# Routed experts after a Fourier filter: weight splits queued one by one, and a penalty added by ScalarE instead of GpSimd

## The chip, the cores and the metric

The kernel runs on one core of a Trainium2 chip. The metric is the device time of one execution in microseconds (us). Engine names are those of the profile: PE (TensorE matmuls), PEld (its weight loads), DVE (VectorE), ACT (ScalarE), POOL (GpSimd), SP (SyncE).

## What is computed

The input `x` (8 x 2496 x 256, float32) is filtered along its sequence in the frequency domain, and the 19968 resulting tokens go through eight experts. Each (token, expert) pair has a logit. Pairs are taken in falling order of their logits, over all tokens and experts at once; a token is given to the expert of the pair if it has none yet and the expert has fewer than 2496 tokens. Then each expert runs two matrix products with a relu between them on its own tokens.

```
y = irfft(rfft(x, axis=1) * (filt_r + 1j*filt_i))       # 8 x 2496 x 256
logits = y @ w_gate                                     # 19968 x 8
for idx in argsort(-logits.flatten()):                  # greedy, capacity 2496 per expert
    tok, e = idx // 8, idx % 8
    if assigned[tok] < 0 and counts[e] < 2496: assigned[tok] = e; counts[e] += 1
out[assigned == e] = relu(y[assigned == e] @ w1[e]) @ w2[e]   # w1: 256x1024, w2: 1024x256
```

## The kernel before

**Stages.** Up to about 530 us the kernel computes the Fourier filter as matrix products (class `Fft`) and the logits `lg`, a tile of 117 x 176 x 8 in SBUF whose last index is the expert. From there on the eight experts run one after another (class `Ffn`, `run`). While expert number e computes, the routing of the next one (class `Route`) is woven into the same instruction streams.

**The experts.** An expert's 2496 tokens come in five groups `g` of 512 (the last of 448). For each group, eight first products (`first`, line 850) write `pz`, a PSUM tile of 128 x 512. Four such buffers exist, and the transposes of gathered tokens (`turn`, `ptr`, line 828) share them. ACT makes the high part of the relu from `pz` (line 856, the relu copy), and DVE the low part (`hl`, lines 864 and 867), which frees the buffer. Each matrix operand is split into a high and a low part in this way, so that three matmuls give the precision of one in full float32. The second products (line 897) sum 24 matmuls into `py` for each 128 tokens; ACT copies `py` to `y` (line 907), and POOL scatters `y` to the output rows (line 908).

**The next expert's weights.** `Ffn.weights` loads both raw matrices by indirect DMAs from POOL (line 793). `split` turns them into high and low parts in eight pieces of 128 x 512 (parts 0 to 3 are of the first matrix, 4 to 7 of the second): ACT casts the high part (line 807; parts 0 to 3 read with a step of 8 elements), then POOL subtracts it from the raw piece (line 808). In `emit` a piece is taken from the list `split` after every fourth step of the expert's program; a step is one `yield` of `run`, and a second product of 128 tokens has four. The list is emptied at the hook `last`, in the last group. A piece's place in the program is not its place in the engine's queue: a scheduler orders the instructions of all engines but PE, and it moves them to where it expects them to be ready.

**The routing of the next expert.** `Route.phase` finds, in eleven rounds of counting, which expert closes next and its threshold. Then DVE computes the penalty `pen` for the closed expert (line 687), and POOL adds it to all logits in one instruction (line 718; 1408 elements per partition); the first reader afterwards is the maximum at line 635. The line is queued after the weight loads (`issue_after(s.wdma)`). The list of tokens is made by `places` in five chunks: DVE prepares bounds (lines 699 to 712, 747) and for each chunk a 0/1 matrix `OH` (lines 748, 749), which PE multiplies with a table (`rt`, line 755). Those matmuls stand at fixed places between the expert's own: PE's order is written by hand (`manual_schedule`), and PE waits where an operand is late.

```python
nc.scalar.copy(hi, src)                                                      # 807
(nc.gpsimd if e or part >= 4 else nc.vector).tensor_tensor(lo, src, hi...)   # 808
if split and n % 4 == 0: W.split(*split.pop(0))                              # 1031
```

Of the kernel before, what the change touches and what calls it, by code (L numbers as in the profile page):

```python
# [16 lines left out]
S = B * G  # L17
# [3 lines left out]

LAGS = [(1.6, 1.2), (1.9, 1.2), (2.4, 1.4), (2.2, 1.3), (2.2, 1.2), (2.6, 1.2), (2.6, 1.2), (2.6, 1.2)]
LO, M0, M1, M7 = (4.2, 1.2, 1.4), 3.5, 4.9, 6.9
TU0, TU = 1.1, 1.15
ORD, TF = (1, 0, 0, 1), (3, 5)
I1, FS, C0 = 5, -1, -4.4
V1, V1D, V2, V3, VP, I2, AC = 8, 0.5, 3, 2, -1, 5, 6.5
# [433 lines left out]
class Route:  # L461
# [166 lines left out]
    def phase(s, ph):  # L628
# [85 lines left out]
        yield 'w', 1.5  # L714
        if ph == 7:
            return
        with s.tc.issue_after(s.wdma) if ph else nullcontext():
            nc.gpsimd.tensor_tensor(s.lg, s.lg, pen[:117].unsqueeze(1).to_broadcast([117, S, 8]), op=OP.add)
        with s.tc.issue_after(s.last):
            t, t3 = v("u", [117, S]), v("u2", [117, S])  # L720
            nc.vector.scalar_tensor_tensor(s.asg, mem, 50.0, s.asg, op0=OP.mult, op1=OP.add)
# [53 lines left out]
class Ffn:  # L775
# [58 lines left out]
    def run(s, e, pump, hook):  # L834
# [7 lines left out]
        def first(g, f):  # L842
            n = min(512, CAP - 512*g)
            xh, xl = s.xT[e, g]
            p = s.ps.tile([128, 512], F32, name="pz", tag="c", bufs=4)
            m = 0
            for k in range(2):
                sl = slice(1024*k+128*f, 1024*k+128*f+128)
                for w, x in ((w1h, xh), (w1h, xl), (w1l, xh)):
                    nc.tensor.matmul(p[:, :n], w[:, sl], x[:, k, :n], start=m == 0, stop=m == 5)  # L850
                    m += 1
                yield 0.65 * n / 512
            hl = s.wp.tile([128, 1024], F32R, name="hl", bufs=NH)
            hs.setdefault(g, []).append(hl)
            h, l = (hl[:, 512*k:512*k+512] for k in range(2))
            nc.scalar.activation(h[:, :n], p[:, :n], AF.Relu)  # L856
            if f % 2 == 1 and f < 7 and 0 < g < 4 and s.busy():
                r = s.wp.tile([128, 512], F32, name="hr", bufs=2)
                nc.scalar.activation(r[:, :n], p[:, :n], AF.Relu)
                nc.gpsimd.tensor_tensor(l[:, :n], r[:, :n], h[:, :n].bitcast(F32), op=OP.subtract)  # L860
            else:

                if g < 4:
                    nc.vector.scalar_tensor_tensor(l[:, :n], p[:, :n], 0.0, h[:, :n].bitcast(F32), op0=OP.max, op1=OP.subtract)  # L864
                else:
                    for a, b, c in ((384, n, n), (0, 384, 512)):
                        nc.vector.scalar_tensor_tensor(hl[:, c:c+b-a], p[:, a:b], 0.0, h[:, a:b].bitcast(F32), op0=OP.max, op1=OP.subtract)
# [13 lines left out]
        for g in range(5):  # L881
            n = min(512, CAP - 512*g)
            yield from firsts(g, 8)
            if g == 4:
                hook('last')
            for t in range(4):
                if g < 4:
                    yield from firsts(g + 1, ORD[t])
                w = min(128, n - 128*t)
                p = s.ps.tile([128, D], F32, name="py", tag="b", bufs=2)  # L890
                half = w == 64
                hi, lo, both = slice(128*t, 128*t+w), slice(512+128*t, 512+128*t+w), slice(384, 512)
                terms = ((both, w2h), (hi, w2l)) if half else ((hi, w2h), (hi, w2l), (lo, w2h))
                m = 0
                for f in range(8):
                    for a, b in terms:
                        nc.tensor.matmul(p[:a.stop-a.start], hs[g][f][:, a], b[:, 256*f:256*f+256],  # L897
                                         start=m == 0, stop=m == 8 * len(terms) - 1, skip_group_check=half)
                        m += 1
                    if f in ((3,) if half else (1, 3, 5)):  # L900
                        yield 0.65
                y = s.wp.tile([128, D], F32, name="y", bufs=4)
                if half:
                    nc.scalar.copy(y[:w], p[w:])
                    nc.vector.tensor_tensor(y[:w], p[:w], y[:w], op=OP.add)
                else:
                    nc.scalar.copy(y, p)  # L907
                st = nc.gpsimd.indirect_dma_start(  # L908
                    out=out_rows, out_offset=bass.IndirectOffsetOnAxis(ap=ids[1][:w, 4*g+t:4*g+t+1], axis=0),
                    in_=y[:w], in_offset=None)  # L910
                for o in s.scat:
                    s.tc.declare_no_dep(st.ins, o.ins, reason="each token has one place")
                s.scat.append(st)
                if t in (1, 2) and g == 4:
                    hook(t)
                yield 0.65


def emit(tc, i, out):
    nc = tc.nc  # L920
    with ExitStack() as st:
# [89 lines left out]
        with tc.issue_after(R.last):  # L1011
            while split:
                W.split(*split.pop(0))
        n = 0
        with tc.manual_schedule(engines={mybir.EngineType.PE}):
            for e in range(8):
                pump.limit = e + 1
                def hook(what):
                    if isinstance(what, tuple):
                        gather(e, what[1])  # L1020
                    elif e < 7:
                        if what == 'last':
                            gather(e + 1, 0)
                            while split:
                                W.split(*split.pop(0))
                        else:
                            W.turn(e + 1, 0, what - 1)
                for pe in W.run(e, pump, hook):
                    pump.feed(pe)
                    n += 1  # L1030
                    if split and n % 4 == 0:
                        W.split(*split.pop(0))


class Pump:
# [80 lines left out]
```

## Time and profile before

| what | value |
|---|---|
| median of 3 runs | 1607.03 us (1606.12 to 1614.62) |
| the profiled execution | 1623.63 us, span 1621.9 us |
| mean granted TensorE clock | 0.944 |
| busy share PE, DVE, ACT, POOL | 88%, 62%, 43%, 40% |

The profile is of one execution that took 1.0% longer than the median of the runs. Times in a timeline count from the first instruction; "idle before" names what ended an engine's idle time. [...]

### The profile page before, as it was taken

To read this page: it belongs to the slowest core of one execution; us is meant where nothing else is said; L and a number is where in the kernel's file an instruction comes from. 1 tells how busy PE (TensorE), PEld (TensorE's weight loads), DVE (VectorE), ACT (ScalarE), POOL (GpSimd) and SP (SyncE) were. 2 spreads that over 40 slices of the span, in tenths; PEclk is the share of its full clock that TensorE was granted. 3 is DMA by queue.
4 is the path that set the end of the run, shared out by engine and by line. 5 is a ranking of instruction groups with operands and counts; after the bars stand their busy time and mean duration, and the time that the engine had idled before them with its cause. 6 is when DMAs were issued, how large, how long until landed. Compare 5 with 4: busy or idle time off the path is not lost. (4 is left out here: it accounts for less than half of the span.)

```text
span 1621.9 us, 27429 instructions
## 1 busy us (share of the span) xinstructions
PE 1435.0 (88%) x10374; PEld 1254.6 (77%) x10374; DVE 1012.4 (62%) x2560; ACT 702.2 (43%) x1647; POOL 643.7 (40%) x624
## 2 busy tenths in 40 slices
PE   2888777899887799899899799799799799999998
PEld 2887667799554588789788688788688688899898
DVE  3667656687447667766966777876886862422322
ACT  4556445566445433442533343442453343533322
POOL 0233212345111643743744554634744633523311
PEclk9999888999889899899999899899899999999999
DMA  9978879736987211110210121111211221111100
GB/s 148 159 111 167 197 166 179 127 79 148 236 262 265 80 35 69 56 43 24 85 56 31 69 64 39 69 46 48 80 43 45 80 88 34 54 41 40 53 27 25
DMA packets 121096, 148.74 MB, mean 92 GB/s; under 512 B 70630, under 2 KB 93756, under 8 KB 118660
## 3 DMA queue, kind: packets, MB, share of 16 engines
q1 hardware_dynamic: 97994, 70.63, 22.0%
q0 software_dynamic: 17840, 60.34, 11.4%
q10 hardware_dynamic: 5129, 16.01, 2.8%
q8 instruction: 82, 1.34, 0.4%
q14 instruction: 51, 0.41, 0.1%
HBM read 84.47 MB, written 62.50 MB: 91 GB/s over the span
## 5 line engine op out<-in xcount | busy, mean ns | idle before, releaser
L897 PE MATMUL py<-w1h,hl 128*128 128x256 f32 x2496 | 491.8, 290 | 23.1 <-DVE hl L864 20.2
L897 PEld LDWEIGHTS py<-w1h,hl 128*128 128x128 f32 x2496 | 408.4, 194 | 27.0 <-DVE hl L864 20.8
L897 PE MATMUL py<-w1l,hl 128*128 128x256 f32 (+1 forms) x1280 | 362.7, 285 | 0.0
L908 POOL DMA_INDIRECT out<-y,oid x160 | 170.5, 1065 | 406.9 <-ACT y L907 358.3
L856 ACT ACTIVATE hl<-pz 128x512 fp32r<-128x512 f32 (+1 forms) x320 | 186.6, 587 | 231.5 <-PE pz L850 192.9
L850 PE MATMUL pz<-xo,w0h 128*128 128x512 f32 (+1 forms) x640 | 268.0, 419 | 10.4 <-DVE hl L864 3.6
L850 PE MATMUL pz<-z,w0h 128*128 128x512 f32 (+1 forms) x640 | 251.0, 392 | 1.2 <-issue 1.0
L850 PE MATMUL pz<-xo,w0l 128*128 128x512 f32 (+1 forms) x640 | 251.4, 393 | 0.0
L897 PEld LDWEIGHTS py<-w1l,hl 128*128 128x128 f32 (+1 forms) x1280 | 245.0, 191 | 1.9
L864 DVE SCALAR_TENSOR_TENSOR hl<-pz,hl 128x512 fp32r<-128x512 f32 x227 | 155.1, 686 | 120.6 <-ACT hl L856 118.0
L814 POOL DMA_INDIRECT xg<-xs,xid x160 | 169.0, 1056 | 123.0 <-PE ptr L828 43.3
L907 ACT COPY y<-py 128x256 f32<-128x256 f32 x152 | 56.6, 372 | 328.0 <-PE py L897 267.4
L850 PEld LDWEIGHTS pz<-xo,w0h 128*128 128x128 f32 x640 | 124.1, 194 | 32.3 <-issue 7.1
L230 POOL TENSOR_TENSOR P<-P 128x256 f32<-128x256 f32 x80 | 59.7, 747 | 205.8 <-DVE P L228 204.8
L850 PEld LDWEIGHTS pz<-xo,w0l 128*128 128x128 f32 x640 | 122.4, 191 | 24.4
L207 PE MATMUL p<-cS,xr 117*128 117x120 f32 x688 | 107.2, 304 | 36.1 <-ACT xr L195 30.7
L850 PEld LDWEIGHTS pz<-z,w0h 128*128 128x128 f32 x640 | 123.6, 193 | 17.5 <-issue 1.5
L215 ACT COPY Y<-p 64x240 f32<-64x240 f32 (+1 forms) x304 | 116.0, 382 | 43.5 <-PE p L207 37.8
L207 PEld LDWEIGHTS p<-cS,xr 117*128 117x128 f32 x688 | 99.2, 219 | 43.2 <-ACT xr L195 30.7
L550 DVE TENSOR_TENSOR Gm<-M,thr 117x1232 bf16<-117x1232 f32 (+2 forms) x80 | 104.4, 1315 | 0.2
L759 ACT ACTIVATE junka<-rt,loc 128x176 bf16<-128x176 f32 x160 | 65.1, 407 | 70.0 <-DVE loc L756 55.4
L222 PE MATMUL p<-cW,Y 128*128 128x128 f32 x640 | 92.6, 280 | 1.9 <-DVE Q L229 1.9
(235 smaller groups left out, 2374.7 us busy)
## 6 DMA issues: line engine op xcount, KB each, us to landing
xt<-x SPq DMA_DIRECT2D x24, 838.5 KB
zd<-zt SPq DMA_DIRECT2D x140, 128.0 KB
z<-zd SPq DMA_DIRECT2D x26, 600.0 KB
xs<-xo SPq DMA_DIRECT2D x12, 585.0 KB
xs<-xo ACTq DMA_DIRECT2D x11, 585.0 KB
xs<-Y ACTq DMA_DIRECT2D x9, 585.0 KB
zd<-zt ACTq DMA_DIRECT2D x20, 128.0 KB
xg<-xs,xid POOLq DMA_INDIRECT x160
```

The costliest lines, as they stand in the source:

```text
L207: s.lastmm = nc.tensor.matmul(p[:, q-q0, :120], xv[:, q-24*h], s.cS1, start=True, stop=True).ins
L215: (nc.vector.tensor_copy if t in ((5,) if b else (1, 3, 5, 7, 9)) else nc.scalar.copy)(dst, src)
L222: nc.tensor.matmul(p[:, k], s.Y1[b][:, 4*g+k, dh*128:dh*128+128], s.cW[:, 4*g+k], start=True, stop=True)
L230: nc.gpsimd.tensor_tensor(P[:, :, :64], P[:, :, :64], P[:, :, 64:], op=OP.subtract)
L550: nc.vector.tensor_tensor(Gm[:, s0:s1, :m], s.M[:, s0:s1].unsqueeze(2).to_broadcast([117, s1 - s0, m]), thr[:117].unsqueeze(1).to_broadcas ...
L759: nc.scalar.activation(s.junka, pr[:, h, :S], AF.Sign, bias=loc[:, c:c+1], scale=-1.0, accum_out=js[:, c:c+1])
L814: s.lastg = s.nc.gpsimd.indirect_dma_start(out=xg[:n], out_offset=None, in_=s.xs, in_offset=bass.IndirectOffsetOnAxis(ap=ids[0][:n, t:t+1] ...
L850: nc.tensor.matmul(p[:, :n], w[:, sl], x[:, k, :n], start=m == 0, stop=m == 5)
L856: nc.scalar.activation(h[:, :n], p[:, :n], AF.Relu)
L864: nc.vector.scalar_tensor_tensor(l[:, :n], p[:, :n], 0.0, h[:, :n].bitcast(F32), op0=OP.max, op1=OP.subtract)
L897: nc.tensor.matmul(p[:a.stop-a.start], hs[g][f][:, a], b[:, 256*f:256*f+256], start=m == 0, stop=m == 8 * len(terms) - 1, skip_group_check ...
L908: st = nc.gpsimd.indirect_dma_start(out=out_rows, out_offset=bass.IndirectOffsetOnAxis(ap=ids[1][:w, 4*g+t:4*g+t+1], axis=0), in_=y[:w], i ...
```

## The change

The penalty at line 718 becomes eight ScalarE instructions, one for each expert's 176 logits, which lie 8 elements apart. It no longer waits for the weight loads. A split is taken after every fifth step instead of every fourth, and each is queued behind the last relu copy or `y` copy that ACT was given (`issue_after(W.lasta)`), so that the scheduler can't put it ahead of that copy. At the hook `last` only the splits of the first matrix are completed; those of the second may wait until the next expert's first group has its eight first products (hook `w2`).

```diff
-TU0, TU = 1.1, 1.15
+TU0, TU, PACE = 1.1, 1.15, 5
@@ Route.phase
-        with s.tc.issue_after(s.wdma) if ph else nullcontext():
-            nc.gpsimd.tensor_tensor(s.lg, s.lg, pen[:117].unsqueeze(1).to_broadcast([117, S, 8]), op=OP.add)
+        for e in range(8):
+            nc.scalar.activation(s.lg[:, :, e], s.lg[:, :, e], AF.Identity, bias=pen[:117, e:e+1], scale=1.0)
@@ Ffn.run
-            nc.scalar.activation(h[:, :n], p[:, :n], AF.Relu)
+            s.lasta = nc.scalar.activation(h[:, :n], p[:, :n], AF.Relu).ins
...
+            if g == 0:
+                hook('w2')
...
-                    nc.scalar.copy(y, p)
+                    s.lasta = nc.scalar.copy(y, p).ins
@@ emit
+        def flush(p):
+            while split and split[0][1] < p:
+                with tc.issue_after(W.lasta):
+                    W.split(*split.pop(0))
...
-                    if isinstance(what, tuple):
+                    if what == 'w2':
+                        flush(8)
+                    elif isinstance(what, tuple):
...
-                            while split:
-                                W.split(*split.pop(0))
+                            flush(4)
...
-                    if split and n % 4 == 0:
-                        W.split(*split.pop(0))
+                    if split and n % PACE == 0:
+                        with tc.issue_after(W.lasta):
+                            W.split(*split.pop(0))
```

PE's order and SP's are the same in both programs. Below, lines behind 885 carry numbers that are higher by 2 in the changed program (907 and 908 are 909 and 910 there).

**POOL, around the change from the third expert to the fourth.** `wr` are the raw weights, `w0l` and `w1l` low parts of the first and second matrix, `out<-y` a scatter, `xg` a gather of tokens. Before:

```order
L793 DMA wr_10029<-moe_w,widx 128x2048
L793 DMA wr_10030<-moe_w,widx 128x2048
L718 TENSOR_TENSOR lg<-lg,pen 117x1408
L908 DMA out<-y,oid 19968x256
L808 TENSOR_TENSOR w0l<-wr_10029,w0h 128x512 x4
L908 DMA out<-y,oid 19968x256
L808 TENSOR_TENSOR w1l<-wr_10030,w1h 128x512 x4
L814 DMA xg<-xs,xid 128x256 x4
```

And in the changed program:

```order
L793 DMA wr_10050<-moe_w,widx 128x2048
L793 DMA wr_10051<-moe_w,widx 128x2048
L910 DMA out<-y,oid 19968x256
L808 TENSOR_TENSOR w0l<-wr_10050,w0h 128x512
L910 DMA out<-y,oid 19968x256
L808 TENSOR_TENSOR w0l<-wr_10050,w0h 128x512 x2
L814 DMA xg<-xs,xid 128x256 x4
L808 TENSOR_TENSOR w0l<-wr_10050,w0h 128x512
L910 DMA out<-y,oid 19968x256
L808 TENSOR_TENSOR w1l<-wr_10051,w1h 128x512
L910 DMA out<-y,oid 19968x256
L808 TENSOR_TENSOR w1l<-wr_10051,w1h 128x512
```

The penalty is gone, and the two blocks of four subtractions now stand in pieces of one or two between scatters and gathers.

**ACT, the same place.** `hl<-pz` are relu copies, `junka` belongs to `places`. Before:

```order
L907 COPY y<-py 128x256 x3
L856 ACTIVATE hl<-pz 128x512
L807 CAST w0h<-wr_10029 128x512 x4
L907 COPY y<-py 128x256
L856 ACTIVATE hl<-pz 128x512
L831 CAST xo<-ptr 128x2x256
L807 CAST w1h<-wr_10030 128x512 x4
L856 ACTIVATE hl<-pz 128x512 x2
```

And in the changed program:

```order
L909 COPY y<-py 128x256 x2
L718 ACTIVATE lg<-lg,pen 117x176 x8
L909 COPY y<-py 128x256
L856 ACTIVATE hl<-pz 128x512
L807 CAST w0h<-wr_10050 128x512
L909 COPY y<-py 128x256
L856 ACTIVATE hl<-pz 128x512
L807 CAST w0h<-wr_10050 128x512
L831 CAST xo<-ptr 128x2x256
L856 ACTIVATE hl<-pz 128x512 x2
L831 CAST xo<-ptr 128x2x192
L856 ACTIVATE hl<-pz 128x512
```

The eight penalty instructions stand in one block ahead of a `y` copy and a relu copy, and the casts follow one at a time.

**ACT, the weights of the last expert, near the end of the sixth.** Relu copies of 128x448 are the sixth expert's last group, those of 128x512 the seventh's first. Before:

```order
L856 ACTIVATE hl<-pz 128x448 x5
L807 CAST w0h<-wr_15672 128x512 x4
L856 ACTIVATE hl<-pz 128x448
L907 COPY y<-py 128x256 x2
```

And in the changed program:

```order
L856 ACTIVATE hl<-pz 128x448 x6
L909 COPY y<-py 128x256 x2
L831 CAST xo<-ptr 128x2x256
L909 COPY y<-py 128x256
L807 CAST w0h<-wr_15721 128x512
L831 CAST xo<-ptr 128x2x256
L906 COPY y<-py 64x256
L856 ACTIVATE hl<-pz 128x512 x3
```

The four casts ahead of the group's last relu copy are gone from there; the first of them now stands behind the group.

## Rows read from the trace of the kernel before

**Rows 1.** PE's waits: who waited for whom, us in total, times, longest.
```profile
PE rt L755 <- DVE OH L749: 23.4, 4, 10.5
PE py L897 <- DVE hl L864: 20.2, 3, 11.1
PE ptr L828 <- DVE hl L864: 11.4, 1, 11.4
...
PE py L897 <- ACT hl L856: 2.8, 2, 2.1
```
**Rows 2.** Timeline of PE: start us, us, line, operation; in brackets idle time before.
```profile
520.46 0.78 PE L755 MATMUL rt<-tab,OH 117*128 117x180 f16 x4 [3.12 <-DVE OH L749]
```
**Rows 3.** Timeline of DVE: start us, us, line, operation, count.
```profile
901.84 2.97 DVE L701 TENSOR_TENSOR pf<-need,pf 117x1 f32<-117x1 f32 x1
904.73 0.26 DVE L707 TENSOR_SCALAR BE<-pf,need 117x1 f32<-117x1 f32 x1
...
913.22 0.75 DVE L749 SCALAR_TENSOR_TENSOR OH<-iota,BC,oa 117x512 f16<-117x512 f16 x1
914.00 5.16 DVE L748 TENSOR_SCALAR oa<-iota,BC 117x512 f16<-117x512 f16 x1
...
919.87 0.68 DVE L864 SCALAR_TENSOR_TENSOR hl<-pz,hl 128x512 fp32r<-128x512 f32 x1
```
**Rows 4.** Timeline of POOL in the same stretch, idle time before and its end.
```profile
901.54 3.24 POOL L718 TENSOR_TENSOR lg<-lg,pen 117x1408 f32<-117x1408 f32 x1
...
906.18 6.58 POOL L808 TENSOR_TENSOR w0l<-wr,w0h 128x512 fp32r<-128x512 f32 x4 [0.21 <-ACT w0h L807]
...
914.10 4.91 POOL L808 TENSOR_TENSOR w1l<-wr,w1h 128x512 fp32r<-128x512 f32 x4
```
**Rows 5.** Timeline of DVE ahead of the first expert, the same lines.
```profile
517.07 0.26 DVE L707 TENSOR_SCALAR BE<-pf,need 117x1 f32<-117x1 f32 x1
...
519.64 0.75 DVE L749 SCALAR_TENSOR_TENSOR OH<-iota,BC,oa 117x512 f16<-117x512 f16 x1
```
**Rows 6.** Windows of 10 us: busy us (x) of PE, PEld, DVE, ACT, POOL; PEclk.
```profile
649.80:659.80 10.00, 9.95 (x61) 9.34 (x62) 7.24 (x13) 5.27 (x16) 9.14 (x7) 0.85 0.04 13
...
789.90:799.90 10.00, 10.00 (x71) 9.86 (x72) 9.53 (x29) 3.00 (x11) 4.99 (x5) 0.86 0.13 41
920.60:930.60 10.00, 9.99 (x42) 7.71 (x43) 6.92 (x25) 4.59 (x13) 0.74 (x1) 0.73 0.01 2
1043.90:1053.90 10.00, 9.99 (x60) 9.59 (x61) 6.53 (x21) 3.12 (x11) 4.39 (x5) 0.76 0.08 26
1172.70:1182.70 10.00, 9.94 (x37) 7.96 (x38) 8.62 (x26) 4.69 (x14) 0.59 (x1) 0.71 0.01 3
1299.30:1309.30 10.00, 9.96 (x59) 9.61 (x60) 5.16 (x25) 3.12 (x11) 2.38 (x3) 0.73 0.08 26
1373.20:1383.20 10.00, 9.99 (x70) 9.77 (x71) 1.79 (x4) 2.29 (x5) 7.00 (x7) 0.84 0.14 45
```
**Rows 7.** Timeline of ACT ahead of the first expert, and late in the sixth.
```profile
517.37 0.58 ACT L390 COPY xo<-pv 117x512 f32<-117x512 f32 x1 [0.62 <-PE pv L389]
...
528.76 4.20 ACT L807 CAST w0h<-wr 128x512 fp32r<-128x512 f32 x4 [2.80 <-DMA wr<-moe_w,widx]
...
1368.38 4.33 ACT L807 CAST w0h<-wr 128x512 fp32r<-128x512 f32 x4 [0.47 <-PE pz L850]
```
**Rows 8.** Groups by line and form: busy us, mean ns of one, idle before.
```profile
L550 DVE TENSOR_TENSOR Gm<-M,thr 117x1232 bf16<-117x1232 f32 x54 | 77.7, 1440 | 0.2
L759 ACT ACTIVATE junka<-rt,loc 128x176 bf16<-128x176 f32 x160 | 65.1, 407 | 70.0 <-DVE loc L756 55.4 <-DVE X L568 4.1 <-DVE t1b L769 3.3
...
L807 ACT CAST w0h<-wr 128x512 fp32r<-128x512 f32 x32 | 35.5, 1183 | 10.6 <-DMA wr<-moe_w,widx 10.1 <-PE pz L850 0.5
...
L807 ACT CAST w1h<-wr 128x512 fp32r<-128x512 f32 x32 | 17.6, 634 | 1.9 <-PE py L897 1.8
```
**Rows 9.** The chain of waits, merged: three second products without a wait.
```profile
1515.76 8.63 PE py L897 x72
```

## The prediction

> **What bounds the kernel now.** I read PE's waits first. From the first expert to the end PE is the bound, since its order is fixed and it waits for little. Four lines hold nearly all that it loses between experts [rows 1]: 23.4 us for `OH`, 20.2 and 11.4 us for `hl`, all three of DVE, and 2.8 us for a relu copy of ACT. One of the four waits for `OH`, 3.1 us, lies ahead of the first expert [row 2], where a gather and the first weights are what ends the stage. So 20.3 + 20.2 + 11.4 + 2.8 = 54.7 us are lost in seven places: one in each of the six experts in which a routing closes, and one late in the sixth, where the last expert's weights are split.
>
> Why DVE is late is seen by laying its timeline beside POOL's at one such place. L701, one element per partition, takes 2.97 us and ends when POOL's penalty ends [rows 3, 4]. A chunk's L748 takes 5.16 us, as long as four subtractions of POOL. The `hl` that PE has been waiting for follows at 919.87 and takes its usual 0.68 us; it was only behind in the queue. From L707 to the end of the first `OH` DVE needs 9.2 us here (904.73 to 913.97), and 3.3 us ahead of the first expert (517.07 to 520.39), where POOL subtracts nothing [rows 3, 5]. Of the 9.2 us one relu part of 0.7 us is DVE's own. So this place loses 2.9 us at L701, 5.2 us in the chain and 4.8 us at the next L748, together 12.9 us, of which PE felt 11.4. POOL's work there is 3.24 us of penalty and 6.58 + 4.91 = 11.5 us of subtractions, in three blocks [rows 4].
>
> [...]
>
> A wait costs a second time: PE then runs at the lower clock for a while. In the 10 us behind the seven waits the granted clock is 0.85, 0.86, 0.73, 0.76, 0.71, 0.73 and 0.84 with PE busy throughout [rows 6], so (1 - clock) x 10 us = 1.5 + 1.4 + 2.7 + 2.4 + 2.9 + 2.7 + 1.6 = 15.2 us. Together 69.9 us is the most that this change can win at these places.
>
> **The penalty.** Seven POOL instructions of 3.24 us go; ACT gets seven times eight instructions of 176 elements. No row has such a one. Nearest from below is `junka`, 176 elements, 407 ns. A cast that reads with the same step of 8 takes 1183 ns against 634 ns for one without [rows 8], and the penalty also writes with it, so twice 407 ns is my upper end: 3.3 to 6.5 us for eight. I take 3.3, because the same number of elements decides more than the step. [...]
>
> On DVE the whole 2.9 us at L701 goes. On ACT the block stands ahead of relu copies. What a block costs there is shown late in the sixth expert: four casts, 4.33 us [rows 7], ahead of the group's last relu copy cost PE 2.1 us [rows 1]. Scaled to 3.3 us that is 1.6; four `pz` buffers cover it where PE is among first products, so I take 1.2 us, bounds 0 and 3.2 (twice the time, twice the price). Six times: 7.2 us. The penalty's reader, the maximum at L635, comes after the places, so its later end costs nothing.
>
> In the first routing ACT is still copying the filter's output. It idled 0.62 us before its last copy [rows 7], and about as much before each of the others around, 1.7 us in all by this estimate; of the eight instructions 1.6 us are left over. They delay the last copy, the weight load behind it, the casts at 528.76 that waited for that load, and PE's start. The 3.1 us that `OH` comes earlier there don't help, since the load is what PE ends up waiting for. I charge 1.6 us; bounds 0 and 4.8.
>
> **The splits.** All eight stay, with their casts and subtractions; they are dealt out. A step is 8.63 / 12 = 0.72 us [row 9] (three second products of four steps each), so one split per five steps is one per 3.6 us, and eight last 29 us. The first matrix is completed at the hook `last` in any case, ahead of the expert that reads it. In the order POOL has pieces of one or two where it had four, with scatters between. DVE's chain to the first `OH` needs 3.3 us plus a relu part, 4.0 us, and L701 starts 4.3 us before the first subtraction (901.84 and 906.18 [rows 3, 4]), so the chain meets one subtraction at most: 0 to 1.6 us, I take half, six times 0.8 = 4.8 us. Later chunks have seconds between them on PE; the 1.6 us that one can lose there is hidden, as the 1.44 us of each `Gm` instruction is [rows 8], which stand between the same `hl` 54 times without appearing in the larger waits. If that cover is gone, the next late thing is an `hl`.
>
> Late in the sixth expert the casts leave the place ahead of the last relu copy. In the new order five of them come after all eight relu copies of the seventh expert's first group; PE then has two tiles of second products, 5.8 us, before it needs ACT. I charge nothing; bound above, the old 2.1 us.
>
> Moved past what: the scatters stand behind one or two subtractions instead of four, so they leave sooner. SP's queue and PE's order do not move.
>
> **The sum.** Of 69.9 us, 7.2 + 4.8 = 12.0 us of waiting stay in six places, 2.0 us each. The wait of 2.1 us cost 1.6 us more by the clock [rows 1, 6]; shorter ones may cost nothing, so I leave 1.6 us to three of the six: 4.8 us. With the first stage, 12.0 + 4.8 + 1.6 = 18.4 us. The gain is 51.5 us: 1623.6 - 51.5 = 1572.1 us for the profiled execution. That execution is 16.6 us above the median of 1607.0 us, so the median becomes 1555.5 us. The bounds: with no waits left 1607.0 - 69.9 = 1537; with 3.2 us of block and 1.6 us of subtraction in each of six (28.8 us), the old clock cost of those six (13.6 us) and 4.8 us in the first stage 1607.0 - 69.9 + 47.2 = 1584.
>
> **Rivals.**
> - *All of it goes.* The blocks on ACT are covered by the `pz` buffers and no subtraction meets the chain: 1537 us. For it: DVE has 9.2 - 3.3 us to win back and PE's waits all name it. Against: ACT is a queue in order. Chance 0.15.
> - *Half stays.* The scheduler places a penalty where `pen` isn't ready, so that ACT's queue stands, and pairs of subtractions remain on POOL, so the change does in part not do what it says: 1607.0 - 35 = 1572, with 1.6 us at the start 1574 us. Chance 0.20.
> - [...] If DVE always has an instruction that wants what POOL holds, bunching doesn't matter, and only the penalty's 3.2 of 14.7 us go: 22% of 69.9 = 15 us, less 7.2 + 1.6 us: 1600 us. Against: the new spacing leaves 3.6 - 1.6 us free each time, and the chain asks for little. Chance 0.06.
> - *Eight meetings instead of one.* Each subtraction catches DVE ahead of an `hl` and PE feels it each time: 11.5 us a place instead of the present 52.6 / 6 = 8.8, so 16 us more over six, 7.2 us from the block, 1.6 us at the start and 4 us more at the lower clock, less 3.7 us late in the sixth: 1632 us. It decides as soon as PE has less than 1.6 us of slack at most `hl`. The 54 `Gm` of 1.44 us speak against that. Chance 0.05.
>
> **How the numbers follow.** The forecast, 1555.5 us, has 0.54, with 1543 to 1569 as its own range. About 0.5%, 8 us, is what a measurement of this kernel can tell from no change. The forecast and the first two rivals lie below 1599 us: 0.89 faster. The third rival lies at the edge: 0.05 of it same, 0.01 faster. Slower is the fourth: 0.05. With 0.01 more for what I don't see on either side that is 0.88, 0.06, 0.06. The range leaves out the third and fourth rival and what of the first comes out below 1535: 1535 to 1582 us, with the bound of 1584 nearly whole.
>
> **What would show it.** Right: L701 at about 0.2 us in every expert; no L748 above 2 us; PE's waits for `OH` and `hl` together under 15 us; the mean granted clock up by about 0.01; the `junka` waits of ACT shorter. L718 on ACT at 0.4 us each: at 0.8 us my price of the block is half. Wrong: if PE waits for `hl` of ACT by more than 10 us, the block is the new bound; if L748 and L749 still take 1.5 us and PE waits for them, the spacing is too tight; if the first `pz` starts over 3 us later, the first stage was underpriced.

## The result and the profile after

The changed kernel takes 1591.18 us (median of 4 runs, 1587.11 to 1598.48) beside 1609.74 us for the kernel before in the same series: ratio 0.9878, 95% interval 0.985 to 0.9906. It is faster by 18.6 us, where 51.5 us were forecast, and lies 9 us above the range. Its profiled execution took 1590.93 us, with a span of 1589.2 us and a mean granted clock of 0.955 (0.944 before).

PE's waits in the experts and for the lists, of the changed kernel (who waited for whom, us in total, times, longest; the line of `ex` includes two waits, 3.8 us, ahead of the first `pz`):

```profile
PE rt L755 <- DVE ex L760: 11.3, 6, 4.7
...
PE ptr L828 <- DVE hl L864: 6.3, 3, 4.6
PE py L899 <- DVE hl L867: 5.7, 4, 2.3
PE pz L850 <- DVE z L832: 5.5, 4, 3.3
PE pz L850 <- DVE hl L864: 5.4, 4, 2.3
...
PE py L899 <- DVE hl L864: 2.3, 1, 2.3
...
PE rt L755 <- DVE OH L749: 0.6, 2, 0.4
```

The seven long waits of [rows 1] are gone: `OH` from 23.4 to 0.6 us, `hl` of L864 at the second products from 20.2 to 2.3 us. In their place stand short waits: from the first `pz` on PE waits 28 times for DVE, 4.7 us at most, and once for ACT. The largest sum is for an instruction that was in no forecast: `ex`, which frees the two `rt` buffers.

The clock followed. Windows of 10 us behind the new waits at the six places where the clock fell, and behind one late in the sixth expert (busy us of PE, PEld, DVE, ACT, POOL; then PEclk, the granted clock as a share of full speed):

```profile
674.40:684.40 10.00, 9.96 (x73) 9.86 (x74) 6.99 (x25) 6.39 (x22) 7.52 (x7) 0.85 0.22 66
806.70:816.70 10.00, 9.84 (x72) 9.07 (x73) 7.53 (x30) 3.11 (x11) 6.92 (x8) 0.83 0.21 63
1015.10:1025.10 10.00, 9.99 (x54) 8.76 (x55) 8.62 (x27) 4.44 (x8) 2.17 (x2) 0.83 0.32 133
1043.50:1053.50 10.00, 9.99 (x40) 7.85 (x41) 9.84 (x23) 5.15 (x17) 5.48 (x6) 0.70 0.14 41
1165.00:1175.00 10.00, 9.87 (x60) 8.92 (x61) 9.77 (x29) 5.14 (x21) 6.27 (x5) 0.83 0.08 28
1284.70:1294.70 10.00, 9.95 (x48) 8.01 (x49) 7.95 (x26) 5.66 (x15) 5.87 (x7) 0.83 0.25 75
1368.60:1378.60 10.00, 9.95 (x78) 9.43 (x79) 5.79 (x24) 5.27 (x20) 4.80 (x5) 1.00 0.11 39
```

(1 - clock) x 10 us is 11.3 us over the six, against 15.2 us in [rows 6]: waits of 1.0 to 4.7 us left about three quarters of the clock's loss. The share is rough, since both sums leave out low stretches beside other waits (0.84 from 666.80 and 0.83 from 685.50 us before, 0.66 from 670.30 us after).

Where DVE stood still shows in its groups by line (busy us, mean ns of one). Of the kernel before:

```profile
L749 DVE SCALAR_TENSOR_TENSOR OH<-iota,BC,oa 117x512 f16<-117x512 f16 x40 | 39.3, 982 | 0.4
L748 DVE TENSOR_SCALAR oa<-iota,BC 117x512 f16<-117x512 f16 x40 | 22.4, 561 | 0.5
L747 DVE TENSOR_SCALAR BC<-BE 117x2 f32<-117x2 f32 x40 | 21.2, 599 | 0.0
L712 DVE SCALAR_TENSOR_TENSOR asg<-eqm,vc,asg 117x176 f32<-117x176 f32 x7 | 17.6, 2518 | 0.0
L701 DVE TENSOR_TENSOR pf<-need,pf 117x1 f32<-117x1 f32 x7 | 17.6, 2512 | 0.1
...
L637 DVE TENSOR_TENSOR tmp<-lg,M 117x1408 f32<-117x1408 f32 x6 | 10.0, 1669 | 0.0
...
L763 DVE TENSOR_SCALAR js<-js 128x4 f32<-128x4 f32 x40 | 7.4, 184 | 0.0
```

The same view of the changed kernel:

```profile
L749 DVE SCALAR_TENSOR_TENSOR OH<-iota,BC,oa 117x512 f16<-117x512 f16 x40 | 38.6, 964 | 0.4
L748 DVE TENSOR_SCALAR oa<-iota,BC 117x512 f16<-117x512 f16 x40 | 25.4, 636 | 0.5
L763 DVE TENSOR_SCALAR js<-js 128x4 f32<-128x4 f32 x40 | 16.4, 411 | 0.0
L637 DVE TENSOR_TENSOR tmp<-lg,M 117x1408 f32<-117x1408 f32 x6 | 12.9, 2144 | 0.0
...
L712 DVE SCALAR_TENSOR_TENSOR asg<-eqm,vc,asg 117x176 f32<-117x176 f32 x7 | 4.0, 570 | 0.0
L747 DVE TENSOR_SCALAR BC<-BE 117x2 f32<-117x2 f32 x40 | 3.6, 160 | 0.0
L701 DVE TENSOR_TENSOR pf<-need,pf 117x1 f32<-117x1 f32 x7 | 1.1, 154 | 0.1
```

The lines ahead of the first `OH` (L701, L712, L747) came free or nearly so: from L701 to the end of the first `OH` DVE takes 3.4 to 8.1 us in the six experts, where it took 9.9 to 18.6 us. The chunks' own lines (L749, L748) are as slow as before, and lines behind them have become slower: L763, and the next routing's L637. One such place, in the fifth expert. DVE (start, us; rows left out are short):

```profile
1156.25 4.78 DVE L637 TENSOR_TENSOR tmp<-lg,M 117x1408 f32<-117x1408 f32 x1
...
1161.58 1.68 DVE L734 TENSOR_TENSOR r<-r,dr 128x8 f32<-128x8 f32 x1
...
1164.83 0.15 DVE L760 TENSOR_SCALAR ex<-rt 128x4 f32<-128x4 f32 x1
```

POOL in the same stretch:

```profile
1156.57 1.73 POOL L808 TENSOR_TENSOR w0l<-wr,w0h 128x512 fp32r<-128x512 f32 x1
1158.25 1.29 POOL L808 TENSOR_TENSOR w1l<-wr,w1h 128x512 fp32r<-128x512 f32 x1
1159.71 2.21 POOL L910 DMA_INDIRECT out<-y,oid  x1 [0.17 <-issue]
1161.95 1.27 POOL L808 TENSOR_TENSOR w1l<-wr,w1h 128x512 fp32r<-128x512 f32 x1
```

And PE:

```profile
1165.03 0.33 PE L755 MATMUL rt<-tab,OH 117*128 117x180 f16 x2 [4.66 <-DVE ex L760]
```

L637 takes 1.61 us at its shortest in the changed kernel, and 1.62 us on average without subtractions (run 5). Here it takes 4.78 us and ends 1.5 us behind POOL's two subtractions, which end at 1159.54. The third ends at 1163.22, 0.04 us ahead of L734, which takes 0.16 us in the median of its seven times in this trace. The small `ex` is behind both in DVE's queue, and PE waits 4.66 us for it.

### The profile page after: what moved, and what is told of

Same layout as the page of the kernel before. It is cut to its first block, busy times and chain, and to the rows that moved or that the text cites. A ratio compares the mean times of both kernels' runs of the same rounds, so it can differ in the third digit from the quotient of the medians.

```text
span 1589.2 us, 27471 instructions
## 1 busy us (share of the span) xinstructions
PE 1422.3 (90%) x10374; PEld 1243.6 (78%) x10374; DVE 997.5 (63%) x2560; ACT 728.1 (46%) x1703; POOL 628.9 (40%) x617
## 4 chain that ended last, share of the span: by engine, by line
PE 62%; DVE 15%; DMA 8%; issue 6%; ACT 4%; SPq 3%; POOL 1%; POOLq 0%; DVEq 0%; ACTq 0%
PE py L899 20%; PE pz L850 20%; PE pa L271 4%; DMA xt<-x 3%; PE p L222 3%; PE pv L386 3%; PE p L207 3%; PE ptr L828 2%; PE rt L558 2%; PE pa L241 2%; DMA z<-zd 2%; SPq L186 1%; ACT lg L718 1%; PE pv L250 1%; DVE hl L864 1%
## 5 line engine op out<-in xcount | busy, mean ns | idle before, releaser
L910 POOL DMA_INDIRECT out<-y,oid x160 | 173.8, 1086 | 377.6 <-ACT y L909 335.6
L864 DVE SCALAR_TENSOR_TENSOR hl<-pz,hl 128x512 fp32r<-128x512 f32 x227 | 155.2, 687 | 129.1 <-ACT hl L856 128.8
L207 PE MATMUL p<-cS,xr 117*128 117x120 f32 x688 | 102.5, 295 | 44.2 <-ACT xr L195 30.5
L207 PEld LDWEIGHTS p<-cS,xr 117*128 117x128 f32 x688 | 94.8, 210 | 50.7 <-ACT xr L195 30.5
L759 ACT ACTIVATE junka<-rt,loc 128x176 bf16<-128x176 f32 x160 | 65.4, 409 | 69.4 <-DVE loc L756 43.3
```

Of the source, the lines that this page charges most:

```text
L207: s.lastmm = nc.tensor.matmul(p[:, q-q0, :120], xv[:, q-24*h], s.cS1, start=True, stop=True).ins
L759: nc.scalar.activation(s.junka, pr[:, h, :S], AF.Sign, bias=loc[:, c:c+1], scale=-1.0, accum_out=js[:, c:c+1])
L910: st = nc.gpsimd.indirect_dma_start(out=out_rows, out_offset=bass.IndirectOffsetOnAxis(ap=ids[1][:w, 4*g+t:4*g+t+1], axis=0), in_=y[:w], i ...
```

## The experiments

Each run is compared with the kernel before on its own chip. Four chips served; the kernel before took 1610.2 us on the first (and about as much where the result was measured) and 1632.2, 1633.6 to 1635.8 and 1628.8 us on the others. Gains are (1 - ratio) x the time of before. "The twelve lines" is the sum of DVE's busy time in L637, L639, L701, L706, L712, L747 to L749, L763, L764, L770 and L771, groups by line of each trace: 174.2 us before, 144.4 us in the changed kernel.

### The two halves

Run 1 is the kernel before, run 4 the changed kernel. Run 2 is the kernel before with this edit alone:

```diff
-        with s.tc.issue_after(s.wdma) if ph else nullcontext():
-            nc.gpsimd.tensor_tensor(s.lg, s.lg, pen[...]...)
+        for e in range(8):
+            nc.scalar.activation(s.lg[:, :, e], s.lg[:, :, e], AF.Identity, bias=pen[:117, e:e+1], scale=1.0)
```

Run 3 is the changed kernel with that edit undone.

> The kernel before, unchanged, profiled anew. The profile that the prediction was read from is of an execution 16.6 us above the median. If its waits are typical, this one shows the same seven places with 50 to 55 us of PE waits for OH, hl and the relu copy behind 534 us, and ends within 5 us of 1622 us. If that execution had more waiting than most, this one shows clearly less, 25 to 40 us, and the expected gain was too large for that reason. Ratio to before 1.000 in either case.

> The penalty goes to ACT, the splits stay as they were before. Theory A (bunched subtractions lock DVE out, each place loses L701's 2.9 us to the penalty and the rest to the splits): 2.9 us of about 12 at each place, so 0.5 to 1% faster less what the block on ACT costs: ratio 0.990 to 1.000. [...] Theory C (the block on ACT eats most of the gain of the splits): slower than before, 1.000 to 1.010.

> The splits are dealt out, the penalty stays on POOL in one instruction of 3.2 us, as before. Theory A: most of the gain is here, ratio 0.985 to 0.992, and L701 still takes 3 us. [...] Theory C: faster than the whole change, 0.975 to 0.985.

> The changed kernel, unchanged, on the same chip as the three others. Ratio 0.985 to 0.991. PE's waits behind the first pz in its profile: about 30 us, as in the first profile of it, now for ex, z and hl.

| first chip | ratio | 95% | gain | twelve lines |
|---|---|---|---|---|
| before again | 1.0007 | 0.9991 to 1.0023 | -1 | 172.8 |
| penalty alone | 0.9896 | 0.9879 to 0.9912 | 17 | 146.5 |
| splits alone | 0.9947 | 0.9929 to 0.9965 | 9 | 168.0 |
| both | 0.9886 | 0.9862 to 0.991 | 18 | 149.3 |

The gain is the penalty's for the larger part, against theory A: alone it gives 17 us where both give 18, and it alone takes much standstill off DVE (the twelve lines fall from 172.8 to 146.5 us). That the length of POOL's hold is the reason is not shown by it, and run 14 below speaks against it. The dealing out takes away 5 us of 173 in the twelve lines, which are a choice. Over everything that DVE does, from the first `pz` to the end, it adds to the standstill. Windows of runs 1 to 4 (busy us of PE, PEld, DVE, ACT, POOL; then PEclk):

```profile
543.76:1612.11 1068.35, 1002.98 (x6971) 897.85 (x6971) 675.23 (x1885) 418.12 (x975) 502.41 (x425) 0.96 0.16 54
540.65:1591.12 1050.47, 1001.63 (x6971) 895.66 (x6971) 649.42 (x1886) 440.76 (x1019) 486.39 (x418) 0.98 0.17 54
538.77:1600.50 1061.73, 1007.42 (x6971) 897.66 (x6971) 688.69 (x1888) 415.61 (x975) 508.56 (x424) 0.98 0.17 54
549.09:1595.42 1046.33, 1003.24 (x6971) 894.43 (x6971) 665.06 (x1886) 439.64 (x1019) 489.47 (x418) 0.98 0.17 54
```

With the same work DVE is busy for 675 us before, 649 us with the penalty alone, 689 us with the splits alone and 665 us with both; without subtractions (run 5) it is 604 us. The dealing out costs DVE 13 and 16 us more standstill and still gains 9 us by itself. By my reading the standstill then falls where PE feels less of it: in these windows PE is idle for 65.4 us in run 1 and 54.3 us in run 3.

### Without subtractions, on another engine, and a longer block on ACT

```diff
 # run 5, Ffn.weights and split, for e > 0
+        lows = [h[1] for h in s.wt[0][1]] if e else [s.ww.tile(...) for k in range(2)]
-        (nc.gpsimd if e or part >= 4 else nc.vector).tensor_tensor(lo, src, hi...)
+        if e == 0:
+            (nc.gpsimd if part >= 4 else nc.vector).tensor_tensor(lo, src, hi...)
 # run 6 (from the change) and run 7 (from run 2)
-        (nc.gpsimd if e or part >= 4 else nc.vector).tensor_tensor(lo, src, hi...)
+        nc.vector.tensor_tensor(lo, src, hi...)
 # run 8, behind the eight instructions
+        for e in range(8):
+            nc.scalar.activation(s.tmp[:, :, e], s.lg[:, :, e], AF.Identity, bias=s.one[:117, e:e+1], scale=1.0)
```

> The changed kernel without POOL's subtractions of the second to eighth expert's weights: those experts use the first expert's low parts, so PE, ACT and the casts do the same work as in the change, and only the 28 + 32 subtractions less the first expert's four are left out. The changed kernel takes about 1593 us on this chip. Theory P (POOL's subtractions still hold up DVE; dealt out, they meet other work of DVE: the product L637, the sums and the hl behind them): of the waits of PE that remain between experts, about 29 us, and the 13 us of lower clock behind them, the larger part goes: 1560 to 1575 us, and L637 takes 1.6 us each time. Theory Q (what remains belongs to DVE's and ACT's own order, the penalty's block on ACT among it): 1585 to 1593 us.

> The changed kernel with all subtractions of weight parts on DVE instead of POOL: the same elements, 1.09 us each for the first matrix by the row of the first expert, about 0.7 us for the second by the hl of the same size, so some 7.2 us of DVE for an expert, where POOL has 12.8 us. Theory P: what counts is how long DVE can't do its own work, so about half of the remaining waits goes: 1575 to 1585 us. Theory Q: no subtraction matters, and DVE only gets more work: 1590 to 1600 us. Rival R (DVE is in order, so a subtraction in its queue also waits for its cast and holds everything behind it, which one on POOL doesn't): slower than the change, above 1600 us.

> The penalty on ACT and all subtractions on DVE, with the splits dealt out as in the kernel before (one per four steps, the scheduler free to move them, the rest at the last group). Theory P: like the run with the splits queued behind ACT's copies, within 6 us of it, since no engine is locked out any more and the bunches cost what they take, 4 x 1.1 us. Rival S (bunches of any engine are what costs): 8 us or more slower than that run.

> The changed kernel with the block of eight penalty instructions on ACT followed by eight more of the same size and step, which write a scratch tile. What the second block adds is what a block of 4.3 us on ACT costs. The prediction's price is 1.2 us for 3.3 us, so 1.6 us each in six places: 10 us more, 1603 us. If ACT has time there, 0 to 3 us more: 1593 to 1596 us. If the price is that of the casts late in the sixth expert (2.1 us for 4.33 us) and the lower clock behind it is paid each time, 22 us more: 1615 us.

| second chip | ratio | 95% | gain | twelve lines |
|---|---|---|---|---|
| no subtractions | 0.9619 | 0.9584 to 0.9655 | 62 | 101.7 |
| subtractions on DVE, dealt out | 0.9722 | 0.9694 to 0.9749 | 45 | 100.4 |
| subtractions on DVE, as before | 0.9834 | 0.9805 to 0.9863 | 27 | 101.3 |
| penalty twice on ACT | 0.9884 | 0.9855 to 0.9913 | 19 | 134.8 |

The times expected were those of the first chip; read against the change's 31 us on another chip of this level (below), the first run gains 31 us more and the second 14 us more, both in the spans of theory P. The subtractions are what is left to win. Without them the twelve lines come down to 101.7 us, taken below as their free length, and with the subtractions on DVE to 100.4 us:

```profile
L808 DVE TENSOR_TENSOR w0l<-wr,w0h 128x512 fp32r<-128x512 f32 x32 | 36.3, 1141 | 10.9 <-ACT w0h L807 10.9
L808 DVE TENSOR_TENSOR w1l<-wr,w1h 128x512 fp32r<-128x512 f32 x32 | 21.5, 684 | 0.1
```

Here (groups by line of run 6) a subtraction takes 1.14 and 0.68 us of DVE; on POOL it takes 1.78 and 1.39 us in the changed kernel. The seventh run came out on rival S's side, 18 us behind the sixth: bunches cost too when POOL has no part in them. Whether it is DVE's four subtractions or ACT's four casts ahead of them this run doesn't tell.

### The change on another chip, late splits, and no elementwise work on POOL

```diff
 # runs 10 (POOL) and 11 (DVE), with PACE = 3
-                    if split and n % PACE == 0:
+                    if split and n % PACE == 0 and (pump.kind in 'GX' or pump.ph > 6):
 # run 12, run 6 and besides
-                    W.busy = lambda: pump.kind in 'GX' and not split
+                    W.busy = lambda: False
```

> The changed kernel again, beside the three other kernels of this batch. If chips differ only in the level of all times, the ratio to the kernel before is 0.986 to 0.991, as in the two series so far. In that case the doubled penalty block (ratio 0.9884 in the batch before) cost at most 0.3%, 5 us. If the ratio is near 0.98, the doubled block cost 14 us.

> The changed kernel with its splits held back until the next routing is in its counting rounds (or, for the last expert, has none), then one per three steps, on POOL as in the change. The first matrix then comes in one bunch of four subtractions at the last group, behind the chunks of the token list and behind L635 to L645. Theory M (what counts is which work of DVE a subtraction meets: the list's chain and the next routing's start, which PE waits for, or the short steps of a counting round): the sum of PE's waits and lower clock in the experts falls from 55 us to 40 to 45 us, ratio 0.975 to 0.982. Theory D (only how long POOL holds DVE counts): ratio 0.986 to 0.991, as the change. Rival: the first matrix comes too late and PE waits for w0l at the start of an expert, up to 5 us each time: ratio above 0.993.

> The same with the subtractions on DVE. Theory M: like the spread subtractions on DVE (ratio 0.972) or up to 0.5% better, since the list's chain and the routing's start are left alone. Theory D: 0.972, no difference. Rival: four subtractions and the casts they wait for stand in DVE's queue ahead of the hl at the end of a group, and PE waits for these: 0.980 or above.

> The subtractions on DVE as in the run with ratio 0.972, and besides no low part of a relu on POOL (L860, 29 times, 1.55 us), all on DVE. POOL then has no elementwise work in the experts. Theory D: DVE is held 29 x 1.55 = 45 us less and works 29 x 0.68 = 20 us more: 0.968 to 0.972. Theory M: these parts stand in counting rounds, where DVE waits for PE anyway (L566 waits 75 us for rt), so POOL's hold costs little there and DVE's own work as little: 0.970 to 0.975. If DVE is the bound there: 0.978 or above.

| third chip | ratio | 95% | gain | twelve lines |
|---|---|---|---|---|
| the change | 0.9812 | 0.9775 to 0.985 | 31 | 145.3 |
| splits late, POOL | 0.9818 | 0.9783 to 0.9853 | 30 | 129.1 |
| splits late, DVE | 0.9713 | 0.9678 to 0.9749 | 47 | 100.1 |
| no elementwise work on POOL | 0.9694 | 0.966 to 0.9728 | 50 | 100.1 |

The change gains 31 us here and not 18, so run 8's ratio, from the chip of a similar level, stands 0.7% or 12 us above the change's: that is the price of a second block of 4.4 us, by a comparison across two chips with some 8 us of noise. It isn't the block's alone: the splits come later behind it, and the twelve lines take 134.8 us in place of 145.3.

Moving the subtractions out of the list's chunks moved the waits and not their sum: PE waits 54 us from the first `pz` on in run 10 and 51 us in run 9. Run 10's ratio lies in theory M's span, but it is the change's own in this series, so it speaks for theory D. In run 10 the twelve lines lose 16 us, but now L568 of the counting rounds is late, and PE waits for that (waits of PE, run 10):

```profile
PE pz L850 <- DVE hl L864: 10.5, 9, 2.2
PE rt L571 <- DVE X L568: 8.3, 8, 3.3
...
PE rt L755 <- DVE t L566: 7.0, 2, 6.6
```

Late or dealt out makes no difference on DVE either (0.9713, and 0.9722 for run 6 on another chip). Run 12 lies in theory D's span, though its interval reaches into theory M's, and beats both kernels: 1.2% under the change in the same series.

### Twice the hold, and the penalty off the chain

```diff
 # run 13
+        if e:
+            nc.gpsimd.tensor_tensor(lo, src, hi.bitcast(F32), op=OP.subtract)
 # run 14, in place of ACT's eight
         with s.tc.issue_after(s.last):
+            nc.gpsimd.tensor_tensor(s.lg, s.lg, pen[...]...)
```

Run 15 is run 2's kernel, run 16 the kernel before.

> The changed kernel with each subtraction of the second to eighth expert's weights done twice on POOL, one behind the other, so that POOL holds DVE for twice as long at the same places. Without them the change gained 31 us more (ratios 0.9619 and 0.9812, two series). Theory D (DVE's standstill grows with POOL's time, and PE pays for it at a steady rate): about 25 to 35 us slower than the change, ratio near 1.00, and the sum of the twelve lines of the list and of the routing's start on DVE rises from 149 us to 185 to 200 us. Theory M (the first subtraction at a place does the harm, or the slack between them covers some): under 12 us slower. Rival: POOL becomes the bound and w0l or w1l come late at the next expert: over 45 us slower.

> The changed kernel with the penalty on POOL as before (one instruction, 3.23 us), but queued behind the first chunk of the token list, so that L701 and the chain to the first OH are free of it. ACT has no penalty. Theory D (the hold counts wherever it stands while the list is made): close to the run with the splits alone, so 9 to 12 us slower than the change. Theory C (its place on the chain, at L701, was what cost): within 4 us of the change, or faster, since ACT is spared the block.

> The penalty on ACT alone, with the weight splits as before, beside the others of this batch. On the first chip its gain was 17 us, the whole change's 18. Theory D: the same relation here: its ratio within 0.003 of that of the change in the series on this chip. If dealing out the splits has a gain of its own that the first chip hid, it is 8 us or more behind the change.

> The kernel before with its own profile in this series, to see where a chip with about 1635 us loses the 25 us against one with 1610 us. If they are in the experts: PE's waits and lower clock there together some 100 us in place of 81. If they are in the filter ahead of them: the first pz starts at about 565 us in place of 544.

| third chip | ratio | 95% | gain | twelve lines |
|---|---|---|---|---|
| each subtraction twice | 1.0178 | 1.0151 to 1.0204 | -29 | 200.2 |
| penalty on POOL, later | 0.9816 | 0.9789 to 0.9843 | 30 | 143.0 |
| penalty alone on ACT | 0.9889 | 0.9863 to 0.9915 | 18 | 145.7 |
| before again | 0.9992 | 0.9973 to 1.001 | 1 | 174.1 |

A doubled hold costs 60 us more than the change (run 9), twice what a steady rate gave. That is where the rival had it, but PE waits for no weight part in this trace. The first 43 us above the free length of the twelve lines cost the change 31 us of run 5's gain; the next 55 us cost 60. So theory D is wrong as a rate. I read it so that part of the standstill is covered by PE's slack, and that this is used up first; no run shows the slack by itself. The chunks and L763 show it (groups by line, run 13), and PE waits 19.5 us for `ex`, where it waited 10.5 us in run 9:

```profile
L749 DVE SCALAR_TENSOR_TENSOR OH<-iota,BC,oa 117x512 f16<-117x512 f16 x40 | 51.0, 1276 | 0.4
L763 DVE TENSOR_SCALAR js<-js 128x4 f32<-128x4 f32 x40 | 36.4, 911 | 0.0
```

Run 15 is 12 us behind the change, so on this chip the dealing out has a gain of its own. Run 16 shows where such a chip loses its time: in the experts, 1091.3 us from the first `pz` at 536.92 us to the end, where run 1 took 1068.3 us.

Run 14 did something other than what was expected of it. The penalty does not stand behind the first chunk in its trace. It only lost its wait for the weight loads, and so it runs ahead of them and starts 1.1 to 6.7 us ahead of L701 in the six experts. In the kernel before the two loads were issued ahead of it, and L701 started within 0.4 us of it in four of the six experts (1.5 us ahead of it and 1.1 us behind it in the others). POOL in the second expert of run 14 (lines behind 718 are one lower in this run):

```profile
774.90 3.25 POOL L718 TENSOR_TENSOR lg<-lg,pen 117x1408 f32<-117x1408 f32 x1
778.30 0.98 POOL L792 DMA_INDIRECT wr<-moe_w,widx  x1 [0.16 <-DVE pf L701]
```

And DVE:

```profile
777.88 0.29 DVE L701 TENSOR_TENSOR pf<-need,pf 117x1 f32<-117x1 f32 x1
```

So the penalty on POOL takes the same 3.22 us, and the kernel equals the change without giving ACT anything. From L701 to the end of the first `OH` DVE takes 3.8 to 5.9 us there. Of L701's 6.5 us below, 2.9 us lie in the first routing and 2.2 us in the first expert:

```profile
L718 POOL TENSOR_TENSOR lg<-lg,pen 117x1408 f32<-117x1408 f32 x7 | 22.5, 3217 | 69.2 <-DVE pen L687 69.0
...
L701 DVE TENSOR_TENSOR pf<-need,pf 117x1 f32<-117x1 f32 x7 | 6.5, 934 | 0.1
```

### The missing half on a chip of the slower level

Run 17 is run 3's kernel, run 18 run 5's.

> The splits queued one by one, the penalty on POOL as before: the half that is missing from the series with 1633 us for the kernel before. There the penalty alone gained 18.6 us and the whole change 31 us. If the two add up, this run gains 10 to 14 us, ratio about 0.992. If the penalty on POOL ahead of L701 spoils the dealing out, it gains 5 us or less, 0.997 or above. If each part alone already frees the same chain, 20 us or more, 0.988. On a chip of the first kind (1610 us) 0.993 to 0.997, as there.

> The changed kernel without POOL's subtractions again (the first expert's low parts serve the others), as a floor beside the run above: 0.960 to 0.964 on a chip with 1633 us. On a chip with 1610 us: if the smaller waits that this kind of chip lacks are no part of what subtractions cost, it gains 40 to 50 us there, 0.970 to 0.975; if it gains the same share, 0.962.

The splits alone have 0.9927 (0.99 to 0.9954), 12 us, and 166.5 us in the twelve lines; no subtractions 0.9588 (0.9565 to 0.9611), 67 us. On chips of this level the parts add up, over two chips: 18 + 12 = 30, and both together gain 31 us. On the first chip they don't: 17 + 9, and both gain 18.

Run 17's kernel and run 14's differ in effect by the penalty's wait for the weight loads alone, and run 14 gains 18 us more, on another chip of this level. Moving the penalty to ACT gained the same 18 us (run 15). So theory C holds: the penalty's place at L701 was what cost, and leaving out that wait is enough to free it.

## Why the prediction was wrong

**The ceiling held.** Without subtractions the gain is 62 and 67 us on two chips. The prediction's 69.9 us less its own 7.2 and 1.6 us for the block on ACT is 61.1 us. The seven places and the lower clock behind them were what POOL cost. They are not nearly all that PE waits for, though: 54.7 us of 75 us from the first `pz` on.

**The price of the penalty's block was about right.** The block of eight takes 1.12 + 0.62 + 2.63 = 4.4 us in ACT's timeline of the first routing (0.64 us for one, partly overlapping, where `junka` with as many elements takes 0.41 us), between the two bounds and above the 3.3 us taken. No run shows the reason given for 3.3 us, that the number of elements decides more than the step. Doubling it costs 12 us across two chips, where the charge scaled to 4.4 us is 8.8 us x 4.4 / 3.3 = 11.7 us; with 8 us of noise and the later splits, the agreement is in part luck. The first stage was charged 1.6 us; `pen` to the first `pz` takes 20.9 us (521.59 to 542.53) where it took 20.3 (513.72 to 533.98). The whole 2.4 us at L701 went, and 2 us at L712 with it. What the prediction didn't see is that the move to ACT wasn't needed: on POOL, but ahead of the weight loads, the penalty does as well (run 14). Its place on the chain was at fault, not the engine. The block on ACT and the early hold on POOL then cost about the same, and no run here prices either by itself.

**The failed step is the splits' charge:** "the chain meets one subtraction at most: 0 to 1.6 us, I take half, six times 0.8 = 4.8 us", and with it "the 1.6 us that one can lose there is hidden". The chain to the first `OH` did come free in the main, as forecast. But all that DVE does for some 25 us behind it was taken as covered: the other chunks, L763, `ex`, the next routing's L637. It isn't. Taking the subtractions away from the dealt-out kernel is worth 62 or 67 us less the 31 us of the change (three chips of the slower level), so 31 to 36 us. Charged were 4.8 us of waiting and, with all of the clock's share, 9.6 us, so 21 to 26 us were missing. The forecast of 51.5 us misses the 31 us of these chips by 20 us. The `Gm` of 1.44 us that were called as evidence stand in counting rounds; the chunks have PE's fixed places for `rt` behind them and two `rt` buffers that `ex` must free.

**The third rival named what happens with the subtractions,** at a chance of 0.06: bunching doesn't matter to how long DVE is held. Above the free length of 101.7 us the twelve lines stood still for 72 us before and for 43 us in the changed kernel, and run 2 without any dealing out has 45 us: the penalty took all of it, and the dealing out next to nothing, or rather added 13 to 16 us over the whole of DVE. For the penalty the rival is wrong: in run 14 POOL's instruction takes as long as before (3217 and 3231 ns), and the kernel gains as much as with the penalty on ACT. The rival's time, 1600 us, was too high since it gave the penalty 22% of the places' loss: alone it brings 17 or 18 us. What of POOL's DVE waits for no run shows; the traces show that DVE's instruction ends with POOL's, L701 with the penalty [rows 3, 4] and L734 with a subtraction in the changed kernel. POOL's own instructions vary too: the dealt-out L808 take 1777 ns each in the first matrix, where bunched ones took 1628 ns; why is open.

**The clock's charge** was a second, smaller miss: 4.8 us for three places, measured 11.3 us at six; it is not to be added to the 31 to 36 us, which contain the clock. "Shorter ones may cost nothing" was half right: behind waits of 1.0 to 4.7 us the granted clock is 0.70 to 0.85 at six places, and 1.00 behind those of 1.7 us (906.90) and 2.1 us (924.70) in the third expert. In the kernel before, the first 2 us behind the wait that ends at 649.85 show 0.50, and 653.80 to 659.80 shows 1.00.

**Late in the sixth expert** nothing was charged. The wait of 2.1 us for a relu copy is gone, and one of 2.3 us for DVE (the single `py` wait for `hl` of L864) stands near there, without a clock cost (1.00 in its window).

**The base.** The gain was worked out on an execution of 1623.6 us and taken off a median of 1607 us in full. That execution resembles those of the slower chips, though its chip isn't on record: from the first `pz` to the end it takes 1087.9 us, run 16 there 1091.3 us, and run 1 on the first chip 1068.3 us. On the slower chips the change gains 31 us. So of the 33 us that are missing, some 12 lie, by this reading, in taking one chip's waits and forecasting for another; why the dealing out brings 12 us on one kind and about 1 us on top of the penalty on the other stays open.

**Its own signs:** L701 at 0.15 us came true, and the clock rose by 0.011. The longest L748 fell from 5.16 to 2.08 us, nearly as forecast, but their mean rose from 561 to 636 ns. `OH` and `hl` sum to 20.3 us, not under 15. The `junka` waits did not get shorter: 69.4 us of idle time, 70.0 us before [rows 8]. As a sign they were a poor choice, since the list was made faster: from L701 to the end of its last `OH` it took 35 to 56 us in the six experts and takes 33 to 49 us now. The first `pz` starts 8.6 us later, over the 3 us that were to mean an underpriced first stage. But `pen` itself comes 7.9 us later, and in three executions of the kernel before it came at 513.7, 516.9 and 520.9 us, so this sign was one of the filter and not of the penalty.

## What to carry to other kernels

Here, spacing out the instructions of one engine that shut out another's changed who was hit more than how long (the twelve lines stand at 168.0 us with the splits alone and at 172.8 us before). So sum the victim's time against its free length before and after, over everything that it does and not only over the chain that was late. Then see what the bound engine feels of it, since here the dealing out cost DVE 13 to 16 us more standstill and still made the kernel up to 12 us shorter. Before work is moved to another engine, ask whether it only waits for something that it doesn't need; here the penalty waited for two loads. And ask whether it can run on the engine that it shuts out; here the subtraction of the first matrix takes 1.14 us on DVE (run 6) and 1.78 us on POOL (the changed kernel), and to have no elementwise work on POOL is worth 1.2% on top of the change. Take the profile for a forecast from an execution that is as long as the median, or scale the gain.

## What was not expected of the hardware

The same program takes 1610 us on one chip and 1629 to 1636 us on three others; one of the three was used at two times and kept its level, the others served once. The seven long waits are alike (for `OH` 21.9 and 23.2 us in runs 1 and 16), but PE's waits for `hl` ahead of `pz` are 0.4 us in one and 8.0 us in the other, spread over all experts. In all PE waits 61 us in run 1 and 79 us in run 16 from the first `pz` on; why is open. The waits of PE, runs 16 and then 1:

```profile
PE pz L850 <- DVE hl L864: 8.0, 7, 2.8
```

```profile
PE pz L850 <- DVE hl L864: 0.4, 1, 0.4
```

The length of a wait does not tell what it costs in clock: 4.66 us at 1165.03 and 1.0 us at 806.7 (with one of 0.8 us shortly ahead of it) each left 0.83 in the window behind them, 2.1 us at 924.70 nothing.
